# q and k in one DRAM tensor per eight heads, with plain-row stores, 48-row fetches and three V tiles moved among the scores

## The chip, the cores and the metric

The kernel runs on one core of a Trainium2 chip. The metric is device time in microseconds (us) of one execution. Three runs of the kernel before gave a median of 1403.66 us (1403.63 to 1404.26).

## The reference

Softmax attention and a SwiGLU feed-forward on the same input are mixed by a gate of one number per row. All is float32; S = 2048 rows, D = 512, H = 32 heads of 16, F = 1792.

```python
def _A_ref(x, wqkv, wo):
    B, S, D = x.shape
    H = 32; Dh = D // H
    qkv = (lambda x, *d: x.transpose(*d))((x @ wqkv).reshape(B, S, 3, H, Dh), 2, 0, 3, 1, 4)
    q, k, v = qkv[0], qkv[1], qkv[2]
    scores = jnp.einsum("bhqd,bhkd->bhqk", q, k) * Dh ** -0.5
    p = _softmax(scores, axis=-1)
    o = jnp.einsum("bhqk,bhkd->bhqd", p, v)
    return (lambda x, *d: x.transpose(*d))(o, 0, 2, 1, 3).reshape(B, S, D) @ wo

def _B_ref(x, w1, w3, w2):
    gate = jnp.einsum("bsd,df->bsf", x, w1)
    up = jnp.einsum("bsd,df->bsf", x, w3)
    return jnp.einsum("bsf,fd->bsd", _silu(gate) * up, w2)

g = _sigmoid((x * gate_w).sum(-1, keepdims=True))
return g * _A_ref(x, wqkv, wo) + (1 - g) * _B_ref(x, w1, w3, w2)
```

## The kernel before, in words

**Numbers.** Most products use pairs of halves: a value is a high half, rounded to the type fp32r, plus the rest (names ending in H and L, or h and l). A product is three matmuls: high by high, high by low and low by high (`three`, L94). For the scores the three are one: a head's K tile has 48 rows (high, high, low; 16 rows each) and its Q tile the matching 48 (high, low, high). Two guard rows (L282) lower every score by a bound, so that the exponential can't overflow. The tiles `Qt` and `Kt` hold a pair of heads, in rows 0 to 49 and 64 to 113.

**Prologue.** TensorE starts with transposes of the identity (`idle`, L353) and then transposes x in four blocks of 512 columns (L165). For each block b, `project_qk(0, b)` (L189) makes q and k of the first eight heads, chunk 0: 24 matmuls (L199), the high half on ScalarE (L203), the low half on VectorE (L204), and `store_qk` (L185) puts the halves in the DRAM tensors `QD`, whose row is 16 * head + d. Between the blocks stand V tiles: `project_v(t)` (L226) makes V of 128 rows by 12 matmuls (`sums_v`, L96 to L98) and a copy on ScalarE. ScalarE also squares the weights (`squares`, L238; VectorE sums them) and x, and `bound` (L245, L246) makes of the sums a bound of all scores and a flag, whether it is small enough; `guard_rows` (L252) writes the bound for every head to the DRAM tensor `M_d` (L262). All engines read the flag (L408) and jump over the branch `row_maxima` (L293), which takes exact maxima instead and is not executed with these inputs. V tiles 13 to 15 are computed ahead of that jump (`last_v`) and copied by VectorE behind it (L415).

**Fetches.** A step is a pair of heads by half of the queries; there are 32. `load_step` (L285) fetches a step's Q, K and guard rows by 6 + 6 + 2 DMAs: three groups of 16 rows for each head (L277, L270) and two guard rows (L282). It is issued 26 scores ahead of the step, on the queue of SyncE (SP), which carries nearly all DMAs. The first step's are issued in the prologue.

**The loop.** The order of the work is a string, written by hand and made of two patterns (below). Q is a score of two heads (L829) with its exponential on ScalarE (L833); P is the product of one score pair with V (L817; 4 units of time); F is a feed (L765): one matmul in each half of the array (rows 0 to 63 and 64 to 127) for the background work. That is a list of blocks (`blocks`, L716): q and k of chunks 1 to 3 (L432), the gate and up products of the feed-forward (L432), its last product (L550), and attention's output product (L634, L641). A block of 12 products takes its 12 matmuls in one half and then, after a turn, 12 in the other, beside those of another block. GpSimd (POOL) splits the weights (`load_weights` L331, `split` L327).

```python
one = "QQFFFFFF" + "QFFF" * 5 + "QPPPP"
two = "QFFF" * 5 + "QPPQQPP"
order = one * LONG + "QQ" + "F" * 7 + two * SHORT + "QFFF" * 5 + "QPPPP"
```

with LONG 90 and SHORT 37: 2467 slots of F.

**Tail.** After the last score the output product of rows 1024 to 2047 lacks the last quarter of the heads (k = 3). `project` (L897) adds it for row tiles 8 to 15, in pairs; tiles 8 and 10 are scaled by the gate on ScalarE and added on GpSimd, the others are mixed on VectorE (`mix`, L646). Each is stored to `out` (L647), 256 KB. SBUF for `wo2`, `wo3`, `od` and `bt0` to `bt2` comes from the pool `wk`, which opens when the prologue's pools close.

## Time and profile before

| what | value |
|---|---|
| median of three runs | 1403.66 us |
| the profiled execution, its own time | 1403.71 us |
| its span, from first to last instruction | 1401.9 us |
| TensorE weight loads (PEld) busy | 826.4 us (59%) |
| ScalarE (ACT) busy | 1034.3 us (74%) |
| VectorE (DVE) busy | 486.9 us (35%) |
| GpSimd (POOL) busy | 329.3 us (23%) |
| main DMA queue (q1) | 111616 packets, 137.92 MB, 41.4% of 16 engines |
| mean granted clock of TensorE | 0.999 |

The profile is of one execution; its times count from the first instruction. A row of the timeline gives the start in us, how long the group took, engine and line, operation, output and inputs, shape, how often; in brackets stands how long the engine had been idle and what ended that. "<-" reads "made from". A line with q behind the engine (SPq) is a DMA being issued, not its transfer. Weight loads overlap the matmuls.

### The profile page before, as it was taken

Reading aid. Unit: us, or ns where it says so; the run is one execution under the profiler, and the core shown is the slowest. Engines: PE = TensorE matmul, PEld = TensorE weight load, DVE = VectorE, ACT = ScalarE, POOL = GpSimd, SP = SyncE. Lnnn points to the kernel's source line nnn. Section 1 sums busy time; section 2 is a strip of 40 time slices with the busy share of each in tenths; the row PEclk is TensorE's granted clock in tenths of the full one; section 3 lists DMA queues with packets and bytes.
Section 4 is the critical chain, followed back from the end, with each engine's and each line's share of the span. In section 5 each row is a group of like instructions: output and inputs, shape, how many; then the busy total and the mean of one; then the engine's idle time right before and its main releaser. Section 6 shows DMA issues by size and latency. Waiting matters only on the chain.

```text
span 1401.9 us, 29019 instructions
## 1 busy us (share of the span) xinstructions
PE 1393.8 (99%) x11497; PEld 826.4 (59%) x11497; DVE 486.9 (35%) x1083; ACT 1034.3 (74%) x1155; POOL 329.3 (23%) x366
## 2 busy tenths in 40 slices
PE   9999999999999999999999999999999999999998
PEld 8866566566566566566566566566555555555554
DVE  5511111564555546555454554511111101111113
ACT  4457677777777777777777777777677887888784
POOL 6123433011011101110110116432344322212312
PEclk9999999999999999999999999999999999999999
DMA  7653554343223423223333236444354453444632
GB/s 209 166 124 94 133 139 113 73 113 77 46 56 85 114 54 76 69 66 93 74 77 74 66 86 165 118 95 91 87 123 105 105 110 77 111 93 110 157 120 78
DMA packets 112479, 141.03 MB, mean 101 GB/s; under 512 B 16276, under 2 KB 70804, under 8 KB 109264
## 3 DMA queue, kind: packets, MB, share of 16 engines
q1 hardware_dynamic: 111616, 137.92, 41.4%
q8 instruction: 93, 1.52, 0.5%
q10 hardware_dynamic: 720, 1.18, 0.2%
q14 instruction: 50, 0.41, 0.1%
HBM read 90.43 MB, written 48.61 MB: 99 GB/s over the span
## 4 chain that ended last, share of the span: by engine, by line
PE 99%; DVE 0%; issue 0%; DVEq 0%
PE acc L817 33%; PE f L432 27%; PE S L829 19%; PE f L550 11%; PE f L634 2%; PE S L199 2%; PE f L641 1%; PE f L96 1%; PE f L98 1%; PE f L97 1%; PE f L165 0%; PE acc L353 0%; PE f L897 0%; PE S L165 0%; PE S L897 0%; DVE xL L646 0%
## 5 line engine op out<-in xcount | busy, mean ns | idle before, releaser
L833 ACT ACTIVATE p<-S 128x1024 f32<-128x1024 f32 x1024 | 967.9, 1026 | 314.1 <-PE S L829 305.0
L817 PE MATMUL acc<-p,V 128*17 128x512 f32 x4096 | 471.5, 594 | 0.0
L829 PE MATMUL S<-Qt,Kt 50*128 50x512 f32 x2048 | 403.7, 407 | 0.8 <-DVE V L415 0.8
L829 PEld LDWEIGHTS S<-Qt,Kt 50*128 50x128 f32 x2048 | 184.0, 184 | 173.5 <-issue 77.7
L817 PEld LDWEIGHTS acc<-p,V 128*17 128x17 f32 x4096 | 103.4, 97 | 275.2 <-issue 275.2
L463 DVE RECIPROCAL sg<-sg 128x64 f32<-128x64 f32 x448 | 209.2, 517 | 52.7 <-issue 49.1
L432 PE MATMUL f<-xH,fl 64*128 64x512 f32 x1088 | 220.6, 395 | 0.0
L432 PE MATMUL f<-xL,fh 64*128 64x512 f32 x1088 | 219.6, 393 | 0.0
L432 PE MATMUL f<-xH,fh 64*128 64x512 f32 x1088 | 218.0, 389 | 0.0
L328 POOL CAST fh<-fr 128x512 fp32r<-128x512 f32 x34 | 22.4, 658 | 428.0 <-DMA fr<-in_B_w_dram 279.6
L432 PEld LDWEIGHTS f<-xH,fh 64*128 64x128 f32 x1088 | 105.6, 184 | 25.0 <-issue 0.4
L432 PEld LDWEIGHTS f<-xL,fh 64*128 64x128 f32 x1088 | 106.4, 186 | 22.5
L432 PEld LDWEIGHTS f<-xH,fl 64*128 64x128 f32 x1088 | 106.1, 186 | 22.7
L789 DVE MEMSET tick<- 1x1 f32 x198 | 11.7, 59 | 281.2 <-PE f L550 143.0
L455 DVE COPY gs<-f 128x512 f32<-128x512 f32 x56 | 38.5, 688 | 65.5 <-PE f L432 59.3
L461 DVE TENSOR_SCALAR sg<-sg 128x512 f32<-128x512 f32 x56 | 27.3, 488 | 88.0 <-ACT sg L460 84.3
L550 PE MATMUL f<-xH,fh 64*128 64x512 f32 x208 | 57.5, 392 | 0.0
L550 PE MATMUL f<-xH,raw 64*128 64x512 f32 x192 | 57.0, 392 | 0.0
L550 PE MATMUL f<-xL,fh 64*128 64x512 f32 x208 | 56.2, 392 | 0.0
L550 PE MATMUL f<-xH,fl 64*128 64x512 f32 x208 | 55.4, 392 | 0.0
L513 POOL CAST fh<-sg 128x512 fp32r<-128x512 f32 (+1 forms) x32 | 18.0, 563 | 147.3 <-DMA sg<-h_d 91.0
L799 DVE COPY u<-acc 128x512 f32<-128x512 f32 x31 | 21.4, 692 | 86.1 <-PE acc L817 86.1
(202 smaller groups left out, 1324.6 us busy)
## 6 DMA issues: line engine op xcount, KB each, us to landing
Kt<-kH_d SPq DMA_DIRECT2D x128, 128.0 KB
h_d<-sg SPq DMA_DIRECT2D x56, 256.0 KB
sg<-h_d SPq DMA_DIRECT2D x43, 256.0 KB
fr<-in_B_w_dram SPq DMA_DIRECT2D x42, 256.0 KB
Qt<-qH_d SPq DMA_DIRECT2D x128, 64.0 KB
Kt<-kL_d SPq DMA_DIRECT2D x64, 128.0 KB
Qt<-qL_d SPq DMA_DIRECT2D x64, 64.0 KB
b_d<-y SPq DMA_DIRECT2D x16, 256.0 KB
```

What stands on the lines that cost most here:

```text
L199: nc.tensor.matmul(ps[:, i, :], w[i][h][:, k, :], xs[b][:, k, :], start=n == 0, stop=n == len(order) - 1)
L328: nc.gpsimd.tensor_copy(hi, src)
L432: return nc.tensor.matmul(ps, w[i == 1][r, k, :], (xL if i == 2 else xH)[b][r, k, :], start=n == 0 and not second, stop=n == 3 * ND - 1 an ...
L455: nc.vector.tensor_copy(gs, ps)
L461: small.append(lambda: nc.vector.tensor_scalar(sg, sg, 1.0, None, op0=OP.add))
L463: small.append(lambda q=q: nc.vector.reciprocal(sg[:, q:q + 64], sg[:, q:q + 64]))
L550: ins = nc.tensor.matmul(ps, hs[t][q][i == 1][r, P * o:P * o + P], (w2L if i == 2 else w2H)[q][r, o, :], start=n == 0 and not second, stop ...
L634: return nc.tensor.matmul(ps, ot[t][i == 1][r, P * k:P * k + P], wo_[k][i == 2][r, :], start=n == 0 and not second, stop=n == 3 * ND - 1 a ...
L799: nc.vector.tensor_copy(u, acc)
L817: nc.tensor.matmul(acc[r:r + DH + 1, :], V[:, k, 2 * j + h, :], p[:, h, :], start=k == 0, stop=k == NT - 1)
L829: nc.tensor.matmul(ps[:, h, :], Kt[i][r:r + 50, P * k:P * k + P], Qt[i][r:r + 50, t:t + 512], start=True, stop=True)
L833: nc.scalar.activation(p, ps, AF.Exp, scale=SCALE)
```

## The change

**Layout of q and k.** For each chunk c of eight heads, q and k (i = 0, 1) lie in one DRAM tensor `QK[i][c]` of 3 x 16 x 8 x 2048: row group o, d, head, time. The row groups are those of the tiles: high, low, high for q and high, high, low for k. The columns of the weights are taken in the order (d, head) when they are split into halves, by a strided read and write (`by_row`, `shaped`), for chunk 0 on GpSimd and VectorE and for chunks 1 to 3 on GpSimd. So a projected block of 128 rows is one row group, and each store is 128 plain rows. A block goes out in 6 stores where it were 4 (each high half twice, each low half once); high halves come first. A step's fetch is 2 + 2 + 2 DMAs: 48 rows of Q, 48 rows of K and 2 guard rows for each head.

**Order of the prologue.** `bound` follows directly on `project_qk(0, 3)`, then V tile 9, `guard_rows`, the first step's fetches of Q, K and guard rows, the last part of the gate, and V tile 10. Tiles 11 and 12 take the place of 13 to 15 ahead of the jump (`EARLY` = 13). Tiles 13 to 15 become the first blocks of the background work (`v_product`, `v_done`), for which the weights of V stay in SBUF (pool `wvp`); LONG is 96 and SHORT 31, 2503 slots of F. The four tiles v0 to v3 of those weights are used again later for `wo2`, `wo3`, `od` and two of the `bt` tiles.

**Last blocks and tail.** Row tile 13's part of the output product is split between the two halves of the array with no turn, as tile 14's was, and the last three blocks wait 3 units for a PSUM bank instead of 7. In the tail each row tile is projected and mixed alone, tile 8 in the middle of tile 15's products; all are mixed on VectorE, and the stores of odd tiles go to ScalarE's queue, of even ones to SyncE's.

The diff without context, cut to what these parts name:

```diff
@@ -128,10 +129,16 @@
+    def by_row(w):
+        return w[:].rearrange("p k (h d) -> p k d h", d=DH)
+    def shaped(w):
+        return w[:].rearrange("p k (d h) -> p k d h", d=DH)
...
-        nc.gpsimd.tensor_copy(wh, w)
-        nc.vector.tensor_sub(wl, w, wh)
+        nc.gpsimd.tensor_copy(shaped(wh), by_row(w))
+        nc.vector.tensor_sub(shaped(wl), by_row(w), shaped(wh))
@@ -177,14 +184,16 @@
-    def x_gate(b):
-        for t in range(4):
+    def x_gate(b, ts=range(4)):
+        for t in ts:
...
-    def store_qk(i, c, b, hi, lo):
-        for t, d in zip((hi, lo), QD[i]):
-            nc.sync.dma_start(d[P * c:P * c + P, 512 * b:512 * b + 512], t.bitcast(F32) if t.dtype == F32R else t)
+    def store_qk(i, c, b, half, t):
+        for o, low in enumerate(((0, 1, 0), (0, 0, 1))[i]):
+            if low == half:
+                nc.sync.dma_start(QK[i][c][o].rearrange("d h t -> (d h) t")[:, 512 * b:512 * b + 512],
+                                  t.bitcast(F32) if t.dtype == F32R else t)
@@ -202,8 +211,9 @@
-        for i in range(2):
-            store_qk(i, c, b, hi[:, i, :], lo[:, i, :])
+        for half, t in ((0, hi), (1, lo)):
+            for i in range(2):
+                store_qk(i, c, b, half, t[:, i, :])
@@ -262,25 +273,22 @@
+    def rows_of(i, hh):
+        return QK[i][hh // 8].rearrange("o d h t -> (o d) h t")[:, hh % 8, :]
...
-            r = 64 * h
-            s = slice(DH * (2 * j + h), DH * (2 * j + h) + DH)
-            for o, ks in enumerate((0, 0, 1)):
-                nc.sync.dma_start(Kt[i][r + DH * o:r + DH * o + DH, :].bitcast(F32), QD[1][ks][s, :])
+            nc.sync.dma_start(Kt[i][64 * h:64 * h + 3 * DH, :].bitcast(F32), rows_of(1, 2 * j + h))
...
-            r = 64 * h
-            s = slice(DH * (2 * j + h), DH * (2 * j + h) + DH)
-            for o, qs in enumerate((0, 1, 0)):
-                nc.sync.dma_start(Qt[i][r + DH * o:r + DH * o + DH, :].bitcast(F32),
-                                  QD[0][qs][s, 1024 * half:1024 * half + 1024])
+            nc.sync.dma_start(Qt[i][64 * h:64 * h + 3 * DH, :].bitcast(F32),
+                              rows_of(0, 2 * j + h)[:, 1024 * half:1024 * half + 1024])
...
-            nc.sync.dma_start(Qt[i][64 * h + 48:64 * h + 50, :].bitcast(F32),
-                              M_d[2 * j + h, :, 1024 * half:1024 * half + 1024])
+            r = 64 * h + 3 * DH
+            nc.sync.dma_start(Qt[i][r:r + 2, :].bitcast(F32), M_d[2 * j + h, :, 1024 * half:1024 * half + 1024])
@@ -335,11 +343,14 @@
+            whole = wh, wl
+            if any(c is chunk for c in chunks[:ND - 1]):
+                wh, wl, r = shaped(wh), shaped(wl), by_row(r)
...
-            out.append((wh, wl))
+            out.append(whole)
@@ -354,12 +365,12 @@
-    nc.gpsimd.tensor_copy(wq[0][0], w0[0])
-    nc.gpsimd.tensor_sub(wq[0][1], w0[0], wq[0][0])
-    nc.gpsimd.tensor_copy(wq[1][0], w0[1])
+    nc.gpsimd.tensor_copy(shaped(wq[0][0]), by_row(w0[0]))
+    nc.gpsimd.tensor_sub(shaped(wq[0][1]), by_row(w0[0]), shaped(wq[0][0]))
+    nc.gpsimd.tensor_copy(shaped(wq[1][0]), by_row(w0[1]))
...
-    nc.vector.tensor_sub(wq[1][1], w0[1], wq[1][0])
+    nc.vector.tensor_sub(shaped(wq[1][1]), by_row(w0[1]), shaped(wq[1][0]))
@@ -393,23 +404,21 @@
     load_weights(chunks[0])
     nc.vector.tensor_reduce(am, x2, axis=AX.X, op=OP.max)
     project_qk(0, 3, wq)
+    bound()
+    project_v(9)
+    guard_rows()
     load_q(0, 0, 0)
-    project_v(9)
-    bound()
+    load_k(0, 0)
+    load_guard(0, 0, 0)
+    x_gate(3)
     project_v(10)
-    guard_rows()
-    load_k(0, 0)
-    project_v(11)
-    x_gate(3)
     nc.scalar.activation(g, z, AF.Exp, scale=-1.0)
     nc.vector.tensor_scalar(g, g, 1.0, None, op0=OP.add)
     nc.vector.reciprocal(g, g)
     nc.vector.tensor_scalar(omg, g, -1.0, 1.0, op0=OP.mult, op1=OP.add)
-    load_guard(0, 0, 0)
-    project_v(12)
     small = nc.values_load(flag, min_val=0, max_val=1)
-    last_v = [sums_v(t) for t in range(NT - 3, NT)]
+    last_v = [sums_v(t) for t in range(11, EARLY)]
     row_maxima(small)
     for to, src in last_v:
         nc.vector.tensor_copy(to, src)
@@ -625,7 +635,11 @@
-        bt[t] = wk.tile([P, 512], F32, name=f"bt{t % 3}")
+        if t == 0:
+            both = wvp.tile([P, 2, 512], F32, name="v3")
+            bt[-3], bt[-2] = both[:, 0, :], both[:, 1, :]
+            bt[-1] = wk.tile([P, 512], F32, name="bt")[:]
+        bt[t] = bt[t - 3]
@@ -713,10 +727,23 @@
+    def v_product(t):
+        b, o = divmod(P * t, 512)
+        def product(ps, r, n, second):
+            k, i = divmod(n, 3)
+            return nc.tensor.matmul(ps, (xL if i == 1 else xH)[b][r, k, o:o + P], wv[k][i == 2][r, :],
+                                    start=n == 0 and not second, stop=n == 3 * ND - 1 and second)
+        return product
+    def v_done(t):
+        return lambda ps: nc.vector.tensor_copy(V[:, t, :, 0:DH], ps.rearrange("p (h d) -> p h d", d=DH))
...
+        for t in range(EARLY, NT):
+            yield v_product(t), v_done(t), 3 * ND
@@ -730,17 +757,19 @@
-        for t in range(NT // 2, NT - 2):
+        for t in range(NT // 2, NT - 3):
...
-        yield part_product(NT - 2, False), (part_done(NT - 2), part_done(NT - 2)), LATE
+        for t in (NT - 3, NT - 2):
+            yield part_product(t, False), (part_done(t), part_done(t)), LATE
...
-    NBLOCK = 8 * len(chunks) + 3 * NT + NT // 2 + NT // 2
+    NBLOCK = NT - EARLY + 8 * len(chunks) + 3 * NT + NT // 2 + NT // 2 + 1
+    FIRST = NT - EARLY + 8 * len(chunks)
...
-    halves = [None, None]
+    halves = [[], []]
@@ -752,14 +781,16 @@
-        if used < 0 or over[used] is not None and over[used] + rest <= clock:
-            block, halves[lane] = halves[lane] or next(source, None), None
+        if used < 0 or over[used] is not None and over[used] + (rest if len(over) < NBLOCK - 3 else 3) <= clock:
+            alone = bool(halves[lane])
+            block = halves[lane].pop(0) if alone else next(source, None)
...
-                    block, halves[1 - lane] = (product, done[0], length), (product, done[1], length)
+                    block, alone = (product, done[0], length), True
+                    halves[1 - lane].append((product, done[1], length))
...
-                return dict(block=block, ps=bank(), id=len(over) - 1, n=0, turn=None, alone=halves[1 - lane] is not None or len(over) == NBLOCK)
+                return dict(block=block, ps=bank(), id=len(over) - 1, n=0, turn=None, alone=alone)
@@ -838,7 +869,7 @@
-    LONG, SHORT = 90, 37
+    LONG, SHORT = 96, 31
@@ -913,7 +944,7 @@
-    project(last, 1, (0, 1))
+    project(last, 1)
@@ -922,35 +953,22 @@
-    project(last, 1, (2,))
-    project(last, 2)
-    def scaled(t):
-        y = wk.tile([P, 512], F32, name=f"p{free[t // 2 - 3]}")
-        nc.scalar.activation(y, banks[t], AF.Copy, scale=g[:, t:t + 1])
-        nc.gpsimd.tensor_add(bt[t], bt[t], y)
-    def store(t):
-        nc.sync.dma_start(out[P * t:P * t + P, :], bt[t])
+    project(last, 2, (0, 1))
...
-    for two in ((8, 9), (10, 11), (12, 13), (14,), (15,)):
-        if two[0] == 12:
+    project(8, k, (0, 1))
+    project(last, 2, (2,))
+    project(8, k, (2,))
+    mix(8, banks[8])
+    for t in range(9, NT):
+        if t == 12:
...
-        for terms in ((0, 1), (2,)):
-            for t in two:
-                project(t, k, terms)
-        for t in two:
-            if t in (8, 10):
-                scaled(t)
-            elif t < last:
-                mix(t, banks[t], nc.scalar if t % 2 == 0 else nc.sync)
-                if t in (9, 11):
-                    store(t - 1)
-            else:
-                mix(t, banks[t], nc.scalar, slice(0, D // 2))
-                mix(t, banks[t], nc.sync, slice(D // 2, D))
+        project(t, k)
+        if t < last:
+            mix(t, banks[t], nc.scalar if t % 2 else nc.sync)
+        else:
+            mix(t, banks[t], nc.scalar, slice(0, D // 2))
+            mix(t, banks[t], nc.sync, slice(D // 2, D))
```

SyncE issues at the end of the prologue, from the stores of the last block on. A row is one or more DMAs; kH_d, qL_d and so on are halves in DRAM, k_d and q_d the new tensors, m_d the guard rows. Before:

```order
L187 DMA kH_d<-hi 128x512
L187 DMA kL_d<-lo 128x512
L277 DMA Qt_108<-qH_d 16x1024
L277 DMA Qt_108<-qL_d 16x1024
L277 DMA Qt_108<-qH_d 16x1024 x2
...
L262 DMA m_d<-sg 32x4x512 x2
L270 DMA Kt_111<-kH_d 16x2048 x2
L270 DMA Kt_111<-kL_d 16x2048
...
L282 DMA Qt_108<-m_d 2x1024 x2
```

And now:

```order
L195 DMA q_d<-hi 128x512 x2
L195 DMA k_d<-hi 128x512 x2
L195 DMA q_d<-lo 128x512
L195 DMA k_d<-lo 128x512
L273 DMA m_d<-sg 32x4x512 x2
L285 DMA Qt_112<-q_d 48x1024 x2
L281 DMA Kt_115<-k_d 48x2048 x2
L291 DMA Qt_112<-m_d 2x1024 x2
```

The stores of a block are six, the write of the guard rows stands ahead of Q, and Q and K are two DMAs each.

TensorE around the bound (L245 and L246, now L256 and L257; f is a PSUM bank, vh, vl and v the weights of V, xH and xL the halves of x). Before, the last rows of V tile 9 and the first of tile 10:

```order
L96 MATMUL f<-vh_226,xH_421 128x512
L97 MATMUL f<-vl_227,xH_421 128x512
L98 MATMUL f<-vh_226,xL_422 128x512
L245 MATMUL f<-rs,V 1x64
L246 MATMUL f<-ident,am 1x128
L96 MATMUL f<-vh_208,xH_421 128x512
```

And now, the last rows of the projection of q and k and the first of V tile 9:

```order
L208 MATMUL S<-xH_592,wl 128x512 x4
L208 MATMUL S<-xL_593,wh 128x512 x4
L256 MATMUL f<-rs,V 1x64
L257 MATMUL f<-ident,am 1x128
L97 MATMUL f<-v_212,xH_425 128x512
L98 MATMUL f<-v_212,xH_425 128x512
```

The bound moved ahead of V tile 9, onto the projection itself.

TensorE in the tail (acc<-ident,p are transposes of the last attention result; wo and v the halves of the output weights; f, S and acc PSUM banks). Before, tile 15's products are finished and then tiles 8 and 9 follow as a pair:

```order
L921 MATMUL acc<-ident,p_21172 128x128 x4
L897 MATMUL f<-xH_15746,xL_20229 128x512
L897 MATMUL f<-wo_17801,xH_20228 128x512 x2
L897 MATMUL f<-wo_17801,xL_20230 128x512
L897 MATMUL S<-wo_17545,xH_20228 128x512 x4
L897 MATMUL S<-wo_17545,xL_20230 128x512 x2
L897 MATMUL f<-wo_17545,xH_20228 128x512 x4
```

And now tile 8 (S) stands between tile 15's last products (f):

```order
L952 MATMUL acc<-ident,p_20804 128x128 x4
L928 MATMUL f<-v_17536,xH_19872 128x512 x2
L928 MATMUL S<-v_17299,xH_19872 128x512 x2
L928 MATMUL f<-v_17536,xL_19874 128x512
L928 MATMUL S<-v_17299,xL_19874 128x512
```

Tile 8's three products are now done before any of tile 9's.

23 lines of the change are left out of this document (13 added, 10 removed).

## The prediction

> **What bounds the kernel now.** I read the page's busy times first, then the waits by engine, then the timelines of TensorE, the DMA queue, ScalarE and VectorE up to 100 us and after 1380 us, and at last the windows for the DMA rates.
>
> ```profile
> PE 1393.8 (99%) x11497; PEld 826.4 (59%) x11497; DVE 486.9 (35%) x1083; ACT 1034.3 (74%) x1155; POOL 329.3 (23%) x366
> PE S L829 <- DVE V L415: 0.8, 1, 0.8
> ```
>
> TensorE (PE) is never free. The second line is from the waits: after its start PE waits once, 0.8 us in front of the first score. So time can only come from what PE executes and from the places where a change opens a gap. There are three such places: the loop's pitch, the stretch before the first score, and the tail.
>
> The loop repeats two patterns of eight score pairs, "one" with 21 F slots and "two" with 15. In the timeline each starts its product with V (L817) at:
>
> ```profile
> 1012.76 3.63 PE L817 MATMUL acc<-p,V 128*17 128x512 f32 x32
> 1023.26 3.63 PE L817 MATMUL acc<-p,V 128*17 128x512 f32 x32
> 1043.43 1.91 PE L817 MATMUL acc<-p,V 128*17 128x512 f32 x16
> 1052.86 1.91 PE L817 MATMUL acc<-p,V 128*17 128x512 f32 x16
> ```
>
> "one" lasts 10.50 us, "two" 9.43 us; both are filled by PE.
>
> **The loop and the moved V tiles.** LONG goes from 90 to 96 and SHORT from 37 to 31: six patterns get 1.07 us longer, **+6.4 us**. The 36 F slots thus bought (six each) hold V tiles 13 to 15, which leave the stretch before the scores. There a tile is 12 matmuls:
>
> ```profile
> 41.94 0.39 PE L96 MATMUL f<-vh,xH 128*128 128x512 f32 x1
> 50.11 0.38 PE L165 MATMUL f<-ident,xn 128*128 128x128 f32 x2
> 62.92 0.27 PE L245 MATMUL f<-rs,V 128*1 128x64 f32 x2
> 80.97 0.93 PE L829 MATMUL S<-Qt,Kt 50*128 50x512 f32 x4 [0.78 <-DVE V L415]
> ```
>
> Three tiles run from 41.94 to 50.11, so 2.72 us each and 8.17 us for three. If the scores could follow the shorter stretch at once, this part would give 8.2 - 6.4 = 1.8 us. That hangs on what the scores wait for, which until now was hidden under just these tiles.
>
> **What the first score waits for.** It needs the low half of k of the last block in DRAM, then K, Q and the guard rows in SBUF.
>
> ```profile
> 61.36 0.34 SPq L187 DMA_DIRECT2D qH_d<-hi  x1
> 63.49 0.45 SPq L187 DMA_DIRECT2D kL_d<-lo  x1
> 68.23 1.88 SPq L270 DMA_DIRECT2D Kt<-kH_d  x2
> 73.37 0.55 SPq L282 DMA_DIRECT2D Qt<-m_d  x2
> ```
>
> The DMA rates are in the windows (last two columns: mean busy share of the 16 engines, GB/s):
>
> ```profile
> 22.00:25.00 3.00, 3.00 (x15) 2.49 (x14) 2.77 (x8) 3.00 (x10) 0.77 (x2) 1.00 0.39 45
> 28.50:35.00 6.50, 6.50 (x38) 5.61 (x37) 0.81 (x2) 2.64 (x5) 6.38 (x12) 1.00 1.09 166
> 35.00:40.00 5.00, 5.00 (x24) 4.09 (x23) 1.70 (x2) 1.75 (x3) 0.01 (x1) 1.00 1.05 310
> 55.00:57.00 2.00, 2.00 (x11) 1.63 (x10) 1.03 (x2) 2.00 (x5) 0.00 (x0) 1.00 0.00 1
> 62.00:67.00 5.00, 5.00 (x25) 3.57 (x24) 1.86 (x7) 1.20 (x2) 0.91 (x1) 1.00 0.91 246
> 72.00:76.00 4.00, 4.00 (x20) 3.30 (x19) 0.00 (x0) 0.60 (x1) 0.00 (x0) 1.00 0.85 121
> 76.00:79.00 3.00, 3.00 (x15) 2.49 (x14) 1.38 (x2) 0.00 (x0) 0.00 (x0) 1.00 0.05 11
> 85.00:89.00 4.00, 4.00 (x37) 2.67 (x37) 0.12 (x2) 4.00 (x5) 0.00 (x0) 1.00 0.98 123
> ```
>
> From 62 to 76 us the engines are full, then quiet: the data of the first step end near 77 us, 3 to 4 us before the first score. PE was busy until about 80.2, so this was hidden. In the changed kernel PE is through earlier. After the last projection of q and k (its end is where a V tile starts at 60.1, which is 62.9 less one tile) stand bound, tile 9, guard, tiles 10 to 12: 4 x 2.72 plus about 1 us of small matmuls, so 72.0. The DMA side changes by three things:
> - A block's hi and lo go out as 6 stores of 256 KB instead of 4: 524 KB more ahead of the K load, which waits for the last of them. At 246 GB/s that is 2.1 us, at 166 (the block-1 stores, 28.5 to 35) 3.2; I take 2.6, between, as the engines get fuller.
> - K comes as 2 fetches of 48 rows instead of 6 of 16. The 786 KB ran at 121 to 123 GB/s with 16 rows (72 to 76, 85 to 89), so 6.4 us. No row has 48; wide 128-partition loads reach 310, so 2.5 us. I take 3.9 us (200 GB/s): -2.5, bounds -3.9 and 0.
> - m_d and Q are issued behind the stores as before.
>
> So the data end again near 77.0 + 2.6 - 2.5 = 77.1 if the stores start as early as now. I don't think they do.
>
> **The stores of the earlier blocks.** ScalarE works in order, and its squares of the weights stand ahead of the copies hi:
>
> ```profile
> 39.41 0.63 ACT L238 ACTIVATE raw<-fr 128x512 f32<-128x512 f32 x1 [2.17 <-DMA fr<-in_A_wqkv_dram]
> 44.16 1.00 ACT L203 ACTIVATE hi<-S 128x1024 fp32r<-128x1024 f32 x1
> 55.31 1.66 ACT L238 ACTIVATE raw<-fr 128x512 f32<-128x512 f32 x3
> 60.31 1.03 ACT L203 ACTIVATE hi<-S 128x1024 fp32r<-128x1024 f32 x1 [0.89 <-PE S L199]
> ```
>
> At 39.41 ScalarE already waits 2.17 us for a weight load that stands behind the stores of block 1. Each block now adds 524 KB to that queue. Block 0's fall into the hole at 22 to 25 (45 GB/s) and cost nothing; without that hole they would cost as block 1's. Block 1's delay the weights of q by 1.7 (310) to 3.2 us (166), taken 2.6, and with them hi of block 2 at 44.16, whose own six stores delay the weights of k by 2.1 to 3.2, taken 2.6. Those had slack: their data ended by 55.0, the third square starts at about 56.4, and hi of block 3 waits 0.89 us for PE; less the landing I count 1.7 us (1.4 to 2.3). So hi of block 3 comes 2.6 + 2.6 - 1.7 = 3.5 us late (1.5 to 5.0). bound now stands on PE directly behind that projection and reads the maxima that ScalarE makes just ahead of hi; so PE waits there too, and tile 12 ends at 72.0 + 3.3 = 75.3.
>
> First score: 77.1 + 3.5 = **80.6**, against 80.97: **-0.4 us**, and a gap of 5.3 us in PE.
>
> **The clock behind that gap.**
>
> ```profile
> 1.55 3.01 PE L353 MATMUL acc<-ident 128*128 128x128 f32 x13 [1.55 <-DVE acc L349]
> 4.90 0.85 PE L165 MATMUL f<-ident,xn 128*128 128x128 f32 x3
> 6.53 0.49 PE L165 MATMUL f<-ident,xn 128*128 128x128 f32 x3
> 1395.73 0.39 PE L897 MATMUL f<-wo,xL 128*128 128x512 f32 x1
> 1396.00:1398.00 2.00, 0.12 (x1) 0.00 (x0) 1.43 (x3) 0.00 (x0) 0.00 (x0) 1.00 1.01 377
> 1398.00:1400.00 2.00, 0.00 (x0) 0.00 (x0) 0.00 (x0) 0.00 (x0) 0.00 (x0) 0.66 0.87 319
> ```
>
> A transpose takes about 0.22 us up to 5.75 and 0.11 from 6.53 on: PE ran at half speed for about 4.4 us after its first matmul. After the last matmul (1396.1) the granted clock falls within 1398 to 1400, a mean of 0.66, so some 2.5 us later. A gap of 5.3 us is twice that; I count 4.4 us at half speed behind it: **+2.2 us** (0 if the gap stays under 2.5; 3.4 at most). The Trainium skill, "TensorE: Matmul & The Clock Gate", Part 1, says that a free-running window of 3.4 us without work halves the clock and a busy one restores it. By that rule the loss is 1.7 to 3.4 us and the sum 1410.7 to 1412.4; the trace's fall after 2.5 us shows that a window need not be wholly empty.
>
> **Strided reads at the start.** The splits of the first weights now read 64 bytes apart on GpSimd.
>
> ```profile
> 7.43 1.29 POOL L358 TENSOR_TENSOR wl<-fr,wh 128x512 fp32r<-128x512 f32 x1
> 9.66 1.08 PE L199 MATMUL S<-xH,wl 128*128 128x512 f32 x4
> 1.25 1.00 POOL L143 MEMSET V<- 128x512 f32 x1
> 24.16 0.53 POOL L146 MEMSET sg<- 128x512 f32 x1 [4.04 <-ACT sg L178]
> ```
>
> The strided memset takes 1.9 times the plain one. With that on the cast ahead and on wl, wl ends near 10.4 and PE waits 0.8 us at 9.66; unchanged, nothing. A gain has no source. Part of it vanishes in the later DMA wait: **+0.3** (0 to 0.8). The Trainium skill, "GPSIMD Engine Reference", Performance pitfalls for Q7 kernels, puts reads at steps over 8 bytes at 1.5 times. By that rule wl ends at about 9.7, PE waits nothing worth counting, and the sum is 1410.9; no row here has such a read.
>
> **The tail.**
>
> ```profile
> 1392.84 0.37 SPq L647 DMA_DIRECT2D out_dram<-xH  x1
> 1394.58 1.41 DVE L646 SCALAR_TENSOR_TENSOR xL<-S,g,xL 128x512 f32<-128x512 f32 x2 [0.38 <-PE S L897]
> ```
>
> Eight output tiles of 256 KB leave between 1392.8 and 1400; 2.1 MB at 377 GB/s are 5.6 us, and the engines are full from 1396 on (above). So the tail ends when the stores started plus 5.6. Tile 8 now goes first on all engines and each mix takes 0.70 us (1.41 for two), as fast as a store. The first store starts about 0.5 us earlier, and the hole behind it (the next two wait for ScalarE and GpSimd) closes: -1.2; one more trailing F slot costs 0.2. **-1.0 us** (-1.4 to 0).
>
> **Edits at no cost.** 14 fetches a step become 6: SP's waits end no wait of PE (second line above), and K and Q are fetched 26 scores ahead. Tiles v0 to v3 stand in for wo2, wo3, od and two bt: their last V product lies 1000 us before. The loop's splits and stores run under PE; if that cover failed, a late K would stop every engine at a step's start. The `halves` lists, FIRST and the rest of 3 only reorder the last few F slots ahead of the tail.
>
> **Sum** against the profiled execution (1403.71 us; span 1401.9 and 1.8 around it; the median of the three runs is 1403.66): -0.4 + 6.4 + 2.2 + 0.3 - 1.0 = +7.5, **1411.2 us**.
>
> **Rivals.**
> - *The earlier stores hide* (hi of block 3 on time): scores at 77.1, so -3.9 instead of -0.4, still a gap of 5 us: +4.0, 1407.7. For it: the hole at 22 to 25. Against: the 2.17 us that ScalarE waits already.
> - *The transfers keep up too*: then VectorE's jump over the untaken branch decides:
>
> ```profile
> 76.72 1.49 DVE L415 COPY V<-f 128x512 f32<-128x512 f32 x2 [5.12 <-DVEq L293]
> ```
>
>  It comes 2.4 us earlier, as guard does: scores at 74.2, -6.8, a gap of 2.2 us without a slower clock: 6.4 - 6.8 + 0.3 - 1.0 = -1.1, 1402.6. It needs stores at the 377 GB/s of the output; only there does a row show that.
> - *Faster*: PE itself sets the start, at 72.0 + 0.8 = 72.8. Then -8.2 + 6.4 - 1.4 = -3.2, 1400.5. It decides only if the scores start before 73.2, so if the jump shrinks as well.
> - *All stores at 166 GB/s*: block 0's cost 3.2 us too, each block 3.2, hi of block 3 is 7.9 us late, and K gains nothing: 77.0 + 3.2 + 7.9 = 88.1, +7.1 us at the start: +15.0, 1418.7.
>
> **How the numbers follow.** A difference under 0.2% (2.8 us) can't be told from none. Chances: my forecast 0.40 (own range 1408 to 1415), the hidden stores 0.24, transfers that keep up 0.20, PE alone 0.10, the slowest 0.06. Slower by over 0.2% (above 1406.5): 0.40 + 0.06 + most of 0.24, and a little off for terms at their low ends: 0.62. Faster (below 1400.9) is the case of PE alone, which lies just there, and the low end of the transfers that keep up: 0.11. Same: the rest, 0.27. The range leaves out the slowest case, most of PE alone and the top of my forecast, together 2 in 10: it runs from the transfers that keep up with the tail at its -1.4 and some of VectorE's jump saved (1401.5) to my forecast with its delays at the upper bounds less a little, since they won't all be there (hi 1.5 later, K 2.5 slower: 1415).
>
> **What would show it.** Right: a gap of PE before the first score of 4 us or more, ended by a DMA, with the score near 80 to 81; ScalarE's squares at 55 and hi at 60 some 3 us later; transposes or scores at half speed after the gap; 96 patterns of 10.50 us. Wrong: the first score before 75 us, no gap of PE, or a loop whose patterns changed length.

## The result

The changed kernel takes 1417.83 us (median of four runs) against 1403.76 before. One of the four took 2594 us at a clock of 0.84 and is left out of all that follows; the other three took 1416.62 to 1418.47, median 1417.19, which is 1.0097 of before, 95% interval 1.0077 to 1.0117. It is slower, as forecast, but by 13.4 us instead of 7.5, and above the range's upper end of 1415.0. The profiled execution took 1418.47 us, its span 1416.5.

### The profile after

The page and the waits of TensorE (what waited, for what; us in total, times, longest):

```profile
PE 1398.2 (99%) x11533; PEld 829.7 (59%) x11533; DVE 490.2 (35%) x1090; ACT 1032.0 (73%) x1151; POOL 330.9 (23%) x364
PE S L860 <- DVE V L424: 6.3, 1, 6.3
PE f L560 <- POOL fr L523: 3.7, 1, 3.7
PE f L266 <- DVE top L260: 1.2, 1, 1.2
PE f L560 <- POOL fr L524: 0.8, 1, 0.8
PE f L560 <- DVE tick L820: 0.4, 1, 0.4
```

Before, TensorE waited once after its start, 0.8 us. Now it waits 1.2 us at the guard rows (L266), which the longer wait behind it hides; 6.3 us at the first score, where 5.3 were predicted, but ended by a DMA; and 4.5 us for GpSimd at L560, the feed-forward's last product, which the prediction did not speak of. To see where the 14.6 us of span came in, I laid the starts of the products with V (L817, now L848) of the two profiled executions side by side; all 4096 are in both:

| stretch (time before) | the changed kernel falls back by |
|---|---|
| start to the first product with V (88.02) | 0.03 |
| to 918 us | -0.1 |
| 918 to 950 us: the wait at L560 | +8.3 |
| 950 to 1034 us | -0.1 |
| six patterns that are longer (1034 to 1100) | +6.9 |
| 1100 to 1386 us | +0.9 |
| from there to the end | -1.4 |

**The start.** The first product with V is the end of the start's account. Before, and then after:

```profile
88.02 3.63 PE L817 MATMUL acc<-p,V 128*17 128x512 f32 x32
```

```profile
79.46 1.42 PE L860 MATMUL S<-Qt,Kt 50*128 50x512 f32 x4 [6.31 <-DVE V L424]
88.04 3.63 PE L848 MATMUL acc<-p,V 128*17 128x512 f32 x32
```

The first score is 1.5 us earlier (79.46 against 80.97), and the first product with V isn't: what lies between took 8.58 us instead of 7.05. The windows show why (the columns are busy time by engine, then granted clock, share of the DMA engines, GB/s):

```profile
74.00:76.00 2.00, 0.00 (x0) 0.00 (x0) 0.00 (x0) 0.00 (x0) 0.00 (x0) 1.00 0.72 111
76.00:78.00 2.00, 0.00 (x0) 0.00 (x0) 0.00 (x0) 0.00 (x0) 0.00 (x0) 0.56 0.10 20
78.00:80.00 2.00, 0.54 (x2) 0.57 (x4) 1.26 (x2) 0.00 (x0) 0.00 (x0) 0.50 0.03 8
82.00:84.00 2.00, 2.00 (x16) 2.00 (x15) 0.00 (x0) 0.95 (x2) 0.00 (x0) 0.73 1.03 184
```

The transfers are through by 76.7, nearly 3 us before the first score, and the clock is at half until it recovers within 82 to 84. So the data did not set the score's start. The wait names VectorE, and its row reads:

```profile
78.74 1.29 DVE L424 COPY V<-f 128x512 f32<-128x512 f32 x2 [8.74 <-DVEq L301]
```

VectorE stands 8.74 us at L301, the jump over the branch `row_maxima`, which isn't executed. It was 5.12 us before. Its first copy behind the jump ends at 79.44. SyncE is hardly earlier: only behind the same jump does it hand on that the first step's DMAs have landed, and the last of these signals is at 79.33. So here two jumps end almost together; the run with the old layout, below, tells them apart.

**The stall.** TensorE, SyncE's queue and GpSimd around it, in the changed kernel:

```profile
938.42 0.40 PE L560 MATMUL f<-xL,fh 64*128 64x512 f32 x1
942.49 0.50 PE L560 MATMUL f<-xH,fr 64*128 64x512 f32 x1 [3.65 <-POOL fr L523]
943.84 0.79 PE L560 MATMUL f<-xH,fr 64*128 64x512 f32 x1 [0.85 <-POOL fr L524]
944.99 6.13 PE L848 MATMUL acc<-p,V 128*17 128x512 f32 x32
```

```profile
922.60 1.12 SPq L836 DMA_DIRECT2D d_d<-u  x4
923.76 2.00 SPq L842 DMA_DIRECT2D o_d<-u  x4
925.86 0.84 SPq L522 DMA_DIRECT2D fr<-in_B_w_dram  x2
...
931.78 0.92 SPq L285 DMA_DIRECT2D Qt<-q_d  x2
932.76 0.88 SPq L281 DMA_DIRECT2D Kt<-k_d  x2
933.68 0.58 SPq L291 DMA_DIRECT2D Qt<-m_d  x2
934.77 10.54 SPq L522 DMA_DIRECT2D sg<-h_d  x4
```

```profile
941.83 0.61 POOL L523 CAST fr<-sg 128x512 fp32r<-128x512 f32 x1 [5.13 <-DMA sg<-h_d]
```

TensorE wants a piece of h, in `fr`, from 938.8 on. GpSimd splits it at 941.83, since its fetch was issued at 934.77 and took 7 us. Just ahead of it on SyncE stands the fetch of a whole step, 1.15 MB, and from 934 to 938 the DMA engines' share is 1.05 and more. Before, GpSimd had this piece long before it was wanted:

```profile
911.80 0.61 POOL L513 CAST fr<-sg 128x512 fp32r<-128x512 f32 x1
```

The product with V behind the gap takes 6.13 us for 32 matmuls that take 3.63 elsewhere: the clock again. From 938.8 to 943.84 less 0.5 of work are 4.5 us of waiting, and most of the rest of the 8.3 is half speed.

**The tail** ends 1.4 us sooner: the stores leave at 1408.30 and from then on at full rate.

```profile
1408.30 1.68 SPq L661 DMA_DIRECT2D out_dram<-xH  x2
1411.00:1413.00 2.00, 1.20 (x6) 0.66 (x4) 2.00 (x4) 0.00 (x0) 0.00 (x0) 1.00 1.01 380
```

### The profile page after: what moved, and what is told of

The parts are those of the page before. It is cut to its first block, busy times and chain, and to the rows that moved or that the text cites. A ratio compares the mean times of both kernels' runs of the same rounds, so it can differ in the third digit from the quotient of the medians.

```text
span 1416.5 us, 28807 instructions
## 1 busy us (share of the span) xinstructions
PE 1398.2 (99%) x11533; PEld 829.7 (59%) x11533; DVE 490.2 (35%) x1090; ACT 1032.0 (73%) x1151; POOL 330.9 (23%) x364
## 3 DMA queue, kind: packets, MB, share of 16 engines
q8 instruction: 92, 1.51, 0.5%
## 4 chain that ended last, share of the span: by engine, by line
PE 92%; DMA 1%; POOL 0%; SPq 0%; issue 0%; DVE 0%; DVEq 0%; POOLq 0%
PE acc L848 32%; PE f L441 27%; PE S L860 19%; PE f L560 10%; PE f L648 2%; PE f L655 1%; PE f L734 1%; DMA dd<-d_d 1%; DMA sg<-h_d 0%; PE f L928 0%; DMA fr<-in_B_w_dram 0%; PE S L928 0%; SPq L842 0%; POOL xL L524 0%; POOL raw L524 0%
## 5 line engine op out<-in xcount | busy, mean ns | idle before, releaser
L848 PE MATMUL acc<-p,V 128*17 128x512 f32 x4096 | 472.9, 597 | 0.0
L848 PEld LDWEIGHTS acc<-p,V 128*17 128x17 f32 x4096 | 104.3, 97 | 279.1 <-issue 277.8
L560 PE MATMUL f<-xH,fh 64*128 64x512 f32 x208 | 58.3, 393 | 0.0
L560 PE MATMUL f<-xL,fh 64*128 64x512 f32 x208 | 56.6, 393 | 0.4 <-DVE tick L820 0.4
L560 PE MATMUL f<-xH,raw 64*128 64x512 f32 x192 | 56.4, 392 | 0.0
L560 PE MATMUL f<-xH,fr 64*128 64x512 f32 x160 | 51.8, 395 | 4.5 <-POOL fr L523 3.7
L560 PE MATMUL f<-xH,fl 64*128 64x512 f32 x208 | 55.5, 394 | 0.0
```

Source lines behind the costliest of these rows:

```text
L560: ins = nc.tensor.matmul(ps, hs[t][q][i == 1][r, P * o:P * o + P], (w2L if i == 2 else w2H)[q][r, o, :], start=n == 0 and not second, stop ...
L848: nc.tensor.matmul(acc[r:r + DH + 1, :], V[:, k, 2 * j + h, :], p[:, h, :], start=k == 0, stop=k == NT - 1)
```

## The experiments

Theory **P** (phase): the three V tiles take 36 F slots at the front, so every later block stands 36 slots later against the steps of 42 us, and the end of the feed-forward meets a step's end and the next one's fetch. Rival **L**: the new layout and its big fetches. Theory **J**: the code behind the jump comes through the same DMA engines as the data. The kernel before was timed again beside the experiments; the four medians are 1403.84, 1403.71, 1403.86 and 1403.59, and each ratio below is to the one taken beside it. Traces are of one execution each.

### All V tiles ahead of the scores again

```diff
-EARLY = 13
+EARLY = 16
-    LONG, SHORT = 96, 31
+    LONG, SHORT = 90, 37
```

with `project_v(11)` and `project_v(12)` back in their places.

> The changed kernel with V tiles 13 to 15 put back ahead of the scores (EARLY = 16, project_v(11) and (12) where they were, LONG 90 and SHORT 37); layout of q and k, fetches, place of the bound and tail stay as changed. Theory P (phase): the stall of 8.3 us between 928 and 950 us of the changed kernel comes from the 36 F slots by which all background blocks are later against the 42 us steps, so it vanishes with them. Then TensorE waits nowhere after its first score, the loop is as long as before, and what is left is the tail's -1.4 and a first score at 80 to 81: 1401.5 to 1403, 0.9985 to 0.9995 of before. Rival L (layout): the fetches of 48 rows, of 1.15 MB in four DMAs, hold up the other transfers wherever they fall, or the reused V tiles hold up GpSimd: a stall of 4 us or more stays near 910 to 950, and the time is 1406 to 1411.

Measured: 1412.45 us, 1.0064 (1.0047 to 1.0081). The stall is gone, and the loop runs as before to within 0.4 us from the first product with V to the last, so P holds on that. But the time didn't come back, since the start lost 7.9 us:

```profile
81.17 0.39 PE L99 MATMUL f<-v,xL 128*128 128x512 f32 x1
86.74 1.42 PE L862 MATMUL S<-Qt,Kt 50*128 50x512 f32 x4 [5.18 <-issue]
```

"issue" means that nothing in the profile held TensorE back. Two later sections look at this (all V tiles ahead with the second fetch later, and the layout alone). The time fits neither expectation.

### The old layout with the rest of the change

```diff
-    QK = [[dram.tile([3, DH, 8, S], F32, name=f"{n}{c}_d") for c in range(ND)] for n in "qk"]
+    QD = [[dram.tile([D, S], F32, name=f"{n}{p}_d") for p in "HL"] for n in "qk"]
```

and with it `store_qk`, `load_k`, `load_q` and the splits as before.

> The changed kernel with the old layout of q and k alone: QD as before, 4 stores a block, fetches of 6 + 6 + 2 DMAs, no permuted columns; V tiles 13 to 15 stay among the scores, LONG 96, SHORT 31, the prologue's order and the tail stay as changed. Theory P: the stall near 930 to 950 stays, 7 to 12 us (14 fetches issue for 2.5 us longer than 6, and stand ahead of the same loads): 1416 to 1421. Rival L: the stall goes and only the loop's +6.4 and the tail's -1.4 are left: 1408 to 1410. The first score tells of the stores too: if the six stores cost anything it comes earlier than 79.46 by 1 us or more; if the jump over the untaken branch sets it, it stays within 1 us.

Measured: 1422.60 us, 1.0138 (1.0121 to 1.0155), 1.6 us above what P expected. The stall is there, 9.9 us; L falls as its cause. With 14 DMAs in a fetch the load of h behind them is issued at 938.30 instead of 934.77 and split at 944.08 instead of 941.83, so the stall is longer.

The first score is at 79.18, but for another reason than in the changed kernel:

```profile
PE S L861 <- SPq L302: 7.4, 1, 7.4
```

VectorE's jump took 2.9 us, and its copies began at 72.08. SyncE was busy issuing the 14 DMAs until 73.1, came through its own jump at 78.25 and gave its last signal at 78.80. So VectorE's jump is not what holds the start in every case, and the equal time says nothing of the six stores.

### One fetch later

```diff
-            if issued % 32 == 6 and step < 2 * NPAIR:
+            if issued % 32 == (20 if issued // 32 == 20 else 6) and step < 2 * NPAIR:
```

> The changed kernel with one fetch moved: the Q, K and guard rows of the step that is fetched at 931.8 us are issued 14 scores later; the other 30 stay. Theory P says in detail that the last loads of h for the second row tile, issued at 934.8, wait 7.0 us because 1.15 MB of that step's fetch were issued just ahead of them. Without it they are issued at about 932 and land 2 to 3 us later, before TensorE needs them at 938.8: no wait of TensorE there, no slower clock behind it, -8.3 us: 1408 to 1410, 1.003 to 1.0045 of before. Rival E: the loads are late because of the 8 stores of the finished heads, issued 922.6 to 925.8 after waiting for the step's last product, so the move gives at most 2.5 us: 1414 to 1417.

Measured: 1410.52 us, 1.0045 (1.0030 to 1.0059). One fetch of 31 in the loop, moved by 14 scores, is worth 6.7 us by the medians and 7.1 between the profiled executions. SyncE, GpSimd and TensorE's waits in this run:

```profile
930.99 9.65 SPq L522 DMA_DIRECT2D sg<-h_d  x5
...
947.21 2.13 SPq L285 DMA_DIRECT2D Qt<-q_d  x2
```

```profile
937.13 0.61 POOL L523 CAST fr<-sg 128x512 fp32r<-128x512 f32 x1 [1.17 <-DMA sg<-h_d]
```

```profile
PE S L860 <- SPq L301: 5.5, 1, 5.5
PE f L560 <- DVE tick L820: 1.0, 1, 1.0
PE f L560 <- POOL fr L524: 0.4, 1, 0.4
```

The piece is split 4.7 us earlier, and the stretch from 918 to 950 costs 1.0 us instead of 8.3. That the fetch stood ahead of these loads is the cause, and the stores of the finished heads (rival E) can't be it alone: they are at their place still. The way it works differs from the expectation, though. The load was to go out at about 932; it went out at 934.05, just after GpSimd had done with an earlier piece, as it did in the changed kernel (934.75 and 934.77). What the fetch had cost is the way to the split: 7.1 us behind it and 3.1 us without it, with the DMA engines' share from 934 to 936 at 1.05 and at 0.40.

### The finished heads' stores later

```diff
         nc.vector.tensor_copy(u, acc)
+        held.append((issued + 8 if issued // 32 == 20 else 0, lambda: evac_out(j, half, u)))
+        release()
```

> The changed kernel with one set of stores moved: the 8 stores of the finished heads that are issued from 922.6 to 925.8 us (after waiting for the step's last product) are issued up to 8 scores later; the fetch at 931.8 stays where it is. Rival E: these stores make the last loads of h late, since everything behind them on SyncE waits for 922 us; then the two loads of w2 go out at about 912 instead of 925.9, and the stall falls by 6 us or more: 1409 to 1412. Theory P in detail (the fetch just ahead of the last loads decides, and a store of h that is ready at 927): the last loads still stand behind that store and the fetch, at 932 to 935, and land near 939 to 942: the stall falls by 0 to 3 us, 1414 to 1418.

Measured: 1415.28 us, 1.0081 (1.0066 to 1.0097). The stretch costs 6.4 us. That is within what P expects:

```profile
914.96 0.86 SPq L522 DMA_DIRECT2D fr<-in_B_w_dram  x2
...
928.60 1.93 SPq L285 DMA_DIRECT2D Qt<-q_d  x2
...
932.14 0.39 SPq L522 DMA_DIRECT2D sg<-h_d  x1
932.87 4.55 SPq L846 DMA_DIRECT2D d_d<-u  x4
```

```profile
PE f L560 <- POOL fr L523: 2.4, 1, 2.4
```

The loads of w2 did go out 11 us earlier, and TensorE still waits for a piece of h. Its load was issued at 932.14, right behind the step's fetch and ahead of the moved stores, and was split at 939.44: 7.3 us again. It isn't a clean test of E all the same, since the moved stores stand in the way of the loads of h that follow, from 940.58 on.

### Two V tiles among the scores

`EARLY` = 14, `project_v(11)` ahead of the gate, LONG 94, SHORT 33. What stands on SyncE now (the order, not a profile):

```
L523 DMA sg<-h_d 128x4x128 x3
L285 DMA Qt_113<-q_d 48x1024 x2
L281 DMA Kt_116<-k_d 48x2048 x2
L291 DMA Qt_113<-m_d 2x1024 x2
```

> The changed kernel with two V tiles among the scores instead of three (EARLY = 14, project_v(11) ahead of the gate, LONG 94, SHORT 33): the background blocks come 24 F slots later than before instead of 36. In SyncE's order the loads of h that were behind the step's fetch in the changed kernel now stand ahead of it. Theory P: the stall at 928 to 950 us is a matter of that place, so it is gone (under 1 us of waiting, no slower clock), and the loop costs 4 patterns of 1.07 us, +4.3; with the last blocks' and tail's -1.4 and a first product with V between 88 and 91: 1406 to 1410. Rival: any V tile among the scores makes the loads late in proportion: a stall of 4 us or more, 1411 to 1414.

Measured: 1405.07 us, 1.0011 (1.0002 to 1.0021), below the expected span of times. TensorE waits nowhere in the loop, and four patterns cost 4.5 us:

```profile
PE S L861 <- SPq L301: 2.8, 1, 2.8
PE acc L364 <- DVE acc L360: 1.6, 1, 1.6
```

24 slots or 36 differ by 12.1 us by the medians. The profiled executions differ by 14.9: the stall is 8.3 of it, the start 3.2, two patterns 2.3, and the stretch near 1110 us 1.1. In this one (1403.80 us, among the fastest of ten that took 1403.13 to 1407.81) the first score came at 77.75 and the clock didn't drop.

### The gap filled

```diff
+    idle(60)
     row_maxima(small)
```

> The changed kernel with 60 transposes of the identity (about 6.5 us of TensorE at full clock) added between V tile 12 and the jump, where TensorE has nothing to do from 73.1 to 79.5 us; nothing else changes. Theory C: the matmuls from 79.5 to about 85 run at half speed because of that gap, and that takes back all of the 1.5 us by which the first score is earlier. With the gap filled the first score stays at 79.5 and the first product with V comes at 86.3 to 86.8 instead of 88.04; the time falls by 1.3 to 1.7 us, 1415.3 to 1416.8. Rival: the clock follows something else than TensorE's work, or the transposes delay TensorE's own jump: first product with V at 88 or later, no gain.

Measured: 1419.84 us, 1.0118 (1.0099 to 1.0136): no gain, since the transposes held back TensorE's own jump (it was through at 81.4 us instead of 76.2). But they tell of the clock, which stays at 1.00 here until the stall near 940:

```profile
81.90 0.93 PE L861 MATMUL S<-Qt,Kt 50*128 50x512 f32 x4 [2.13 <-DMA Qt<-m_d]
88.96 3.63 PE L849 MATMUL acc<-p,V 128*17 128x512 f32 x32
```

From first score to first product with V are 7.06 us, as before (7.05), against 8.58 in the changed kernel. So the half clock cost 1.5 us there.

### The jump ahead of the fetch

```diff
-    load_q(0, 0, 0)
-    load_k(0, 0)
-    load_guard(0, 0, 0)
...
     row_maxima(small)
+    load_step(0)
```

> The changed kernel with the first step's fetch (Q, K, guard rows) behind the jump over the untaken branch instead of ahead of it; the guard rows are still written ahead of it. Theory J: the jumps of VectorE and SyncE take 8.1 and 6.9 us in the changed kernel (4.5 and 3.3 before, 2.9 and 3.6 with the old layout), because the code at the jump's end comes through the same DMA engines behind 1.15 MB of Q and K. With the fetch behind it they take under 5 us; but the fetch is then issued at 71 to 74 instead of 66.6 and lands at 77 to 80, so the first score stays between 77.5 and 81, and the time within 3 us of the changed kernel. Rival: the jumps take 7 to 8 us by themselves; the first score comes at 82 to 85 and the time grows by 3 to 6 us.

Measured: 1421.98 us, 1.0128 (1.0112 to 1.0143), first score at 81.75, 4.8 us slower than the changed kernel. Those are nearly the rival's figures, but not by its mechanism. The jumps, from the branch to the next instruction, in us (worked out from the instructions' times in the traces):

```
                      VectorE   SyncE
before                  4.5      3.3
changed                 8.1      6.9
old layout              2.9      3.6
jump ahead of fetch     2.8      3.2
```

With no fetch queued ahead of it the jump takes 3 us, and J holds for these engines in kind. But the jumps vary from one execution to the next: three other runs with the changed kernel's prologue up to the jump (one fetch later, stores later, gap filled) give 5.5 to 7.6 us for VectorE and 3.5 to 6.1 for SyncE, and three with the prologue of before 4.7 to 5.3 and 3.0 to 4.0. ScalarE passed the same jump in 0.13 us in all of them; why it needs no more can't be seen. What the early jump gave, the fetch took back: it was issued at 72.8 to 76.1, with the second step's right behind it, and TensorE waited 9.7 us for its last rows.

### All V tiles ahead, the second fetch later

```diff
-            if issued % 32 == 6 and step < 2 * NPAIR:
+            if issued % 32 == (20 if issued < 32 else 6) and step < 2 * NPAIR:
```

> The kernel with all V tiles ahead of the scores, and the second step's fetch issued at score 20 instead of 6. In the run with all V tiles ahead TensorE stood still from 81.6 to 86.7 us with nothing to wait for but its own instructions, while that fetch (1.15 MB, issued 79.4 to 81.8) filled the DMA engines, and ran at half speed until 91. Theory J: TensorE's code, too, was queued behind the fetch. Without it the first score comes at 81 to 82.5, no slower clock follows, the first product with V is at 88 to 89.5, and with the tail's -1.4 the time is 1401.5 to 1404, 0.998 to 1.000 of before. Rival: the pause belongs to that order of the code; it stays, and the time is 1410 to 1413.

Measured: 1407.12 us, 1.0022 (1.0013 to 1.0031): 5.3 us better than without, and 3 us worse than J expected. The pause shrank from 5.2 us to 2.8, and the clock stayed up:

```profile
83.86 0.94 PE L862 MATMUL S<-Qt,Kt 50*128 50x512 f32 x4 [2.81 <-issue]
```

The traces list the packets by which instructions are fetched, but not for which engine. Those of 16384 bytes I take for TensorE's: they carry 1.51 of the 1.90 MB of instructions, and TensorE has 23252 of the 28807 instructions. The last ones before it goes on, start and length:

```
all V tiles ahead            83.65  1.57 us     TensorE goes on at 86.74
... second fetch later       81.65  0.96 us                        83.86
layout alone (below)         83.96  1.33 us                        86.77
```

In each of the three TensorE goes on 1.3 to 1.5 us after the packet has landed, and no wait of its own stands in between. That fits a wait for its own code, but doesn't show it. The second step's fetch delays the packet by 2 us, and with the clock this costs 5 us. The remaining 2.8 us are there with the DMA engines idle (share 0.03 and less). In the kernel before such a packet runs from 80.41 to 81.54, and the first score starts at 80.97 all the same; its code may be cut at another place. That stays open.

### The layout alone

The kernel before, with `QK`, `store_qk`, the fetches and the splits of the change, and nothing else.

> The kernel before with the layout of q and k alone: permuted columns, 6 stores a block, fetches of 2 + 2 + 2 DMAs; order of the prologue, V tiles, loop, last blocks and tail as before. Theory J: the code behind the jump and the first step's data share the DMA engines; TensorE's instructions are the same as before, so its code has no new place to wait, and the deeper queue can only make the jumps longer. VectorE's and SyncE's jumps take 5 to 8 us, as VectorE's did in the changed kernel, and TensorE, busy to 80.2, hides most of it: first score at 80.5 to 82.5, nothing in the loop (the 14 fetches of a step were no wait of TensorE): 1403 to 1405.5. Rival: the big fetches hold up TensorE's code in any case, as in the run with all V tiles ahead: a pause of 3 to 5 us at the first score, half speed behind it, 1408 to 1412. If the six stores or the strided reads of the weights cost anything, it is seen here before 60 us.

Measured: 1409.73 us, 1.0039 (1.0024 to 1.0054): the rival's figures. J's corollary, that TensorE's code would meet nothing new, falls.

```profile
86.77 0.79 PE L839 MATMUL S<-Qt,Kt 50*128 50x512 f32 x1 [5.89 <-DMA Qt<-m_d]
```

```profile
82.00:84.00 2.00, 0.00 (x0) 0.00 (x0) 0.00 (x0) 0.00 (x0) 0.00 (x0) 1.00 0.99 168
84.00:86.00 2.00, 0.00 (x0) 0.00 (x0) 0.00 (x0) 0.00 (x0) 0.00 (x0) 0.94 0.76 135
```

The row names a DMA, but the first step's transfers were through by 76.6; the engines are full with the second step's, and the code packet starts at 83.96. In the kernel before, whose 14 fetches SyncE issues one by one from 79.15 on, the engines have room in the same window:

```profile
82.00:84.00 2.00, 2.00 (x20) 1.86 (x18) 0.00 (x0) 2.00 (x3) 0.00 (x0) 1.00 0.46 127
```

The loop gains nothing from 6 DMAs a step instead of 14, and loses next to nothing: +0.3 us. In the changed kernel, where TensorE is done with its V tiles by 73.15, no such pause stands at the first score.

### The tail alone, and with the last blocks

The kernel before with the changed tail:

> The kernel before with the changed tail alone (tile 8 in the middle of tile 15's products, each tile projected and mixed alone, odd tiles stored from ScalarE's queue); prologue, layout, loop and last blocks as before. In all runs with the changed tail so far the end came 15.0 us after the last product with V began, against 16.4 before. If the tail alone does that: -1.2 to -1.4 us, 1402.2 to 1402.7, 0.999 of before. If the end is helped by the new last blocks (row tile 13 split between the halves of the array, banks free after 3 units), it is less: -0.9 to 0.

Measured: 1404.13 us, 1.0002 (0.9993 to 1.0011). From the last product with V to the end are 17.04 us, 0.7 more than before: both expectations missed. With the last blocks of the change as well (`blocks`, `pick`, `halves`):

> The kernel before with the changed last blocks and tail: row tile 13's part of the output product split between the halves of the array without a turn, the last three blocks' banks free after 3 units, and the tail as in the run of the tail alone. There the end came 17.0 us after the last product with V began, in all kernels with both 15.0, before 16.4. If the two belong together: -1.4 us, 1402.2 to 1402.6, 0.999 of before, the fastest of all. If the 15.0 came from the V tiles or the 36 more F slots as well: 1403 to 1404.5.

Measured: 1403.56 us, 1.0000 (0.9991 to 1.0009), 15.29 us to the end in the profiled execution. By the two traces the two belong together, for -1.1 us; the time is the second expectation's, and the timed runs, from 1402.14 to 1405.64, don't show a gain. What spreads them was not looked for.

### The tensors of q and k further apart

The kernel before with 128 unused rows in each tensor of `QD`:

```diff
-    QD = [[dram.tile([D, S], F32, name=f"{n}{p}_d") for p in "HL"] for n in "qk"]
+    QD = [[dram.tile([D + 128, S], F32, name=f"{n}{p}_d") for p in "HL"] for n in "qk"]
```

> The kernel before with the four DRAM tensors of q and k 5 MiB apart instead of 4 (128 unused rows each); all else as before. The stores of block 1 and the weights behind them run at 166 GB/s from 28.5 to 35 us before and with the old layout (167), at 325 and 323 with the new one, at the same busy share of the DMA engines; a packet of 2048 bytes takes 218 ns against 108, though a store's own pattern (128 rows of 2048 bytes, 8192 apart) is the same. Theory A: the distance of the tensors written at once decides, so the rate rises to 280 GB/s or more, and nothing else changes, since no engine waited for these stores long: 1403 to 1404.5, 0.999 to 1.0005 of before. Rival: the order (both high halves first) or something else of the new layout decides, and the rate stays under 200 GB/s.

Measured: 1403.74 us, 1.0000 (0.9991 to 1.0010), with the rate of theory A. The window, with the weights behind the stores, in the changed kernel and then in this run:

```profile
28.50:35.00 6.50, 6.50 (x38) 5.64 (x37) 0.84 (x2) 2.67 (x5) 6.37 (x12) 1.00 1.07 325
```

```profile
28.50:35.00 6.50, 6.50 (x39) 5.61 (x38) 0.71 (x2) 2.54 (x5) 6.38 (x12) 1.00 1.08 371
37.24 1.66 ACT L238 ACTIVATE raw<-fr 128x512 f32<-128x512 f32 x3
```

ScalarE's wait of 2.17 us ahead of its squares is gone, and the kernel is no faster: TensorE had covered it. A packet of 2048 bytes takes 89 ns here and some 210 in the same window of the kernel before. The distance isn't all of it: there the stores of blocks 2 and 3 go to the same four tensors, and their packets take 84 and 97 ns (45 to 49 and 62 to 65 us). What else block 1 needs to be slow was not looked for. That the tensors lie 4 MiB apart is taken from their size; the traces hold no addresses.

## Why the prediction was wrong

**The step that failed** is the loop's term, +6.4 us for "The loop and the moved V tiles". It priced the 36 F slots by the length of the patterns, and that was right: 6.9 measured. What it put at nothing, without a word, is the shift that these slots give to every later block. With it the end of the feed-forward moved into the fetch of a step: TensorE needed a piece of h whose load shared the DMA engines with 1.15 MB, and that was +8.3 us. Moving this one fetch took 7.1 of them away. "Edits at no cost" could not see it, because it asks only whether PE waits for the step's fetch ("SP's waits end no wait of PE"), and not what the fetch slows down. Its claim that 14 fetches may become 6 held in the loop: the stall is there with 14 as well (9.9 us), and the layout alone adds 0.3 us. Of the 14.6 us between the profiled executions 6.2 are left without the stall, 1.3 less than forecast. The rival with all stores at 166 GB/s, at 1418.7, is near the measured time by accident: nothing of its mechanism is in the traces.

**The rest of the loop**: another 0.9 us came near 1110 us, where a turn waited 0.4 us behind VectorE's other work; the other half was not traced.

**The stores** were wrong. Six of them in the new layout don't delay the weights: ScalarE's squares waited less and hi of block 3 came on time.

```profile
38.60 0.63 ACT L249 ACTIVATE raw<-fr 128x512 f32<-128x512 f32 x1 [1.41 <-DMA fr<-in_A_wqkv_dram]
60.23 1.03 ACT L212 ACTIVATE hi<-S 128x1024 fp32r<-128x1024 f32 x1 [0.88 <-PE S L208]
```

The prediction took the 166 GB/s of block 1's stores for a limit of such stores. It is gone when the tensors are 1 MiB longer. The K of 48 rows, put at 200 GB/s, ran from 72 to 76 at 133 against 121 before; the two errors met, and the data ended near 76 as they had.

**The first score** was put at 80.6 and came at 79.46, a right time for a wrong reason: the jumps of VectorE and SyncE, not the transfers or a late hi. That the gap came out near its size (6.3 us for 5.3) is luck too. The rival in which VectorE's jump decides had the right kind of mechanism and 74.2 us as its time: it took the jump's length as fixed and left out SyncE's. VectorE's jump grew from 4.5 to 8.1 us in the profiled executions; with the fetch behind it, it took 2.8. The Trainium skill, "Runtime: NRT & Kernel Launch", Instruction fetch mechanics, says that a taken branch out of the fetched pages forces a fetch of the target page by DMA before the engine goes on; the traces agree in kind, with 2.8 to 3.2 us where no fetch is queued ahead of the jump and 3.5 to 8.1 where 1.15 MB is.

**The clock** was right in kind: 1.5 us for +2.2. The traces give the half clock as 6.83 us from 76.26 to 83.08, of which 3.6 lay on work. The Trainium skill, "TensorE: Matmul & The Clock Gate", Part 1, speaks of free-running windows of 3.4 us, and the traces agree: ahead of the tail, half clock lasted 3.41, 6.83 or 10.24 us in these runs. The length of a gap alone doesn't decide: one of 2.83 us left the clock up (two V tiles among the scores), and one of 2.42 us took it down (stores later, from 939.55 on), though it is shorter than such a window. So the prediction's lower bound, no loss from a gap under 2.5 us, doesn't hold.

**The strided reads** cost nothing, for +0.3 us in the sum: wl ended at 9.46, just ahead of its first use at 9.51.

```profile
7.88 1.58 POOL L369 TENSOR_TENSOR wl<-fr,wh 128x512 fp32r<-128x512 f32 x1
9.51 1.21 PE L208 MATMUL S<-xH,wl 128*128 128x512 f32 x4
```

The cast took 1.08 us for 0.61, the subtraction 1.58 for 1.29. The Trainium skill, "GPSIMD Engine Reference", Performance pitfalls for Q7 kernels, says 1.5 times; the two lie on either side of it.

**The tail** was right in size (-1.4 for -1.0), for a reason that holds by half: in the traces the tail alone makes the end 0.7 us later, and only with the new last blocks does it come earlier.

## What to carry to other kernels

When work is inserted ahead of a long queue of other work, the price isn't only the work: ask for every later hand-over which period it now meets, and for the loads that end a stage which transfers share the DMA engines with them. A fetch that nobody waits for still slows the loads issued behind it, and it lengthened the jumps too. Here one fetch moved by 14 scores gave back 7.1 of 14.6 us, and two tiles instead of three 14.9, between profiled executions; no version beat the kernel before by more than its runs spread.

## What the runs showed of the hardware

- Instructions come through the DMA engines that the data use. A jump of VectorE or SyncE took 2.8 to 3.2 us with no fetch ahead of it and 3.5 to 8.1 us behind a fetch of 1.15 MB; TensorE stood 5.2 to 5.9 us at its first score while such a fetch ran and 2.8 us with the engines idle, which fits a wait for 16384 bytes of code.
- A load of 256 KB issued right behind a fetch of 1.15 MB was ready after 7.1 to 7.3 us, and after 3.1 us without the fetch.
- Stores of block 1 to four tensors of 4 MiB: 166 GB/s and some 210 ns for a packet of 2048 bytes; to tensors of 5 MiB: 371 GB/s and 89 ns. The page's busy share was 1.09 and 1.08, so a full share says nothing of the rate.
- TensorE's clock fell to half in a gap of 2.42 us in one place and stayed up through one of 2.83 us in another.
